# Half of a symmetric score matrix computed, the other half turned by the DMA crossbar: gated attention followed by a low-rank mixer

## The chip, the cores and the metric

One core of one Trainium2 chip runs the whole program. The metric is the device time of one execution in microseconds (us), smaller is better.

Engine names in the profile: PE is TensorE's matmuls, PEld its weight loads (which overlap matmuls), ACT is ScalarE, DVE is VectorE, POOL is GpSimd, SP is SyncE. A name with q (SPq, POOLq) is that engine's sequencer, which issues DMAs. L75 is a line of the kernel's file.

## The reference, cut to what matters

```python
# per batch of 8; S = 3136, D = 256, d_qk = 64, rank 32, hidden 1024
scores = (1 / S) * z @ z.T                 # symmetric
attn   = np.maximum(scores, 0) ** 2        # elementwise: symmetric too
x      = u * (attn @ v)
h      = (x.T @ U @ V).T                   # low rank, along the sequence
y      = x + h
out    = y + np.maximum(y @ w_ch1, 0) @ w_ch2
```

S is 24.5 tiles of 128, padded to 25. Each batch has an attention stage and a mixer stage.

## The kernel before

z, v and the weights are loaded as fp32 and cast by ScalarE. z and, later, x are transposed by matmuls with the identity. All 25 x 25 score blocks are computed, because the attention matmul needs each block with its contraction index on the partitions:

```python
for gi, (g0, gw) in enumerate(igroups):          # 512 query columns at a time
    for jp in range(0, NT, 2):
        for jj in range(npair):
            nc.tensor.matmul(out=ps_s[:, jj, :gw], lhsT=zzT[:, (jp+jj)*P : (jp+jj+1)*P],
                             rhs=zzT[:, g0 : g0 + gw], start=True, stop=True)
        # ReLU: 3 of 4 on ScalarE, 1 of 4 on VectorE; then the square on VectorE
    for q0 in range(0, gtiles, 2):
        for qq in range(nq):
            for jt in range(NT):
                nc.tensor.matmul(out=ps_o[:, qq, :], lhsT=attn_sb[:, jt, q*P : (q+1)*P],
                                 rhs=v_bf[:, jt, :], start=(jt == 0), stop=(jt == NT - 1))
        # x_bf = ps_o * u
...
# mixer: transpose x on TensorE and add V.T t1 in the same PSUM bank
for db in range(ND):
    for q in range(ctiles):
        nc.tensor.matmul(out=ps_u2[:, db, q*P : (q+1)*P],
                         lhsT=x_bf[:, it, db*P : (db+1)*P], rhs=ident, start=(q == 0), stop=False)
    nc.tensor.matmul(out=ps_u2[:, db, :cw], lhsT=t1_sb[:, db*P : (db+1)*P],
                     rhs=V_bf[:, c0 : c0 + cw], start=False, stop=True)
nc.scalar.copy(out=u2T_bf[:, :, c0 : c0 + cw], in_=ps_u2[:, :, :cw])
# then, per 512 columns: up (w1, ReLU on ScalarE) and down (w2)
```

## Time and profile before

| | before |
|---|---|
| median | 1374.6 us |
| TensorE matmuls busy | 1317.1 of 1373.0 us |
| first matmul | 19.7 us |
| one batch later on, attention + mixer | 106.2 + 61.7 us |
| issue of DMAs by SyncE | 288 plain loads and stores of 0.37 us each (median) |

Lines of the page of the kernel before: the span, each engine's busy time with its share of the span, two of the rows in which the span is cut in 40 slices (in tenths), and the shares of the chain of waits that ended last.

```profile
span 1373.0 us, 22895 instructions
PE 1317.1 (96%) x9865; PEld 913.3 (67%) x10008; DVE 707.9 (52%) x1104; ACT 792.9 (58%) x976; POOL 23.7 (2%) x41
...
PE   3999999999999999999999999999999999999998
...
DMA  9611421124111241111411115111121111111101
...
PE 75%; ACT 21%; DMA 2%; issue 1%; DVE 1%; ACTq 0%; SPq 0%; POOL 0%
```

TensorE is full in all slices but the first and the last, and the DMA engines are nearly empty outside loads.

Pieces of the chain that ended last, in order of time (start, length, what):

```profile
154.69 3.78 ACT relu_sb L277 x4
...
162.39 0.86 PE ps_1642 L270 x4
...
210.53 3.06 PE ps_2069 L202 x28
```

A matmul of 256 columns costs 3.06 / 28 = 0.109 us, one of 512 columns 0.86 / 4 = 0.215 us. In the same trace, matmuls of 128, 256 and 512 columns that follow one another without a gap start 55.5, 109.2 and 215.5 ns apart. So TensorE is paid per column streamed, 0.417 ns each, plus 2 to 3 ns a matmul.

Two stretches of the kernel before, attention and mixer of batch 1 (stretch, length, busy time of each engine with its instruction count, the granted clock, the DMA engines' busy share, GB/s), and its longest TensorE wait (total, times, longest):

```profile
196.90:303.10 106.20, 104.98 (x786) 74.18 (x797) 78.61 (x123) 55.35 (x69) 0.31 (x1) 1.00 0.10 29
303.10:364.80 61.70, 59.34 (x449) 39.69 (x455) 9.88 (x16) 42.61 (x53) 1.89 (x3) 1.00 0.40 123
```

```profile
PE ps_124 L128 <- ACT z_bf L121: 19.7, 1, 19.7
```

The attention starts of batches 1 and 7 lie at 196.9 and 1205.9 us in the timeline, so a batch takes (1205.9 - 196.9) / 6 = 168.2 us, and 1373.0 - 8 x 168.2 = 27.7 us lie outside eight such batches: the start and the end.

### The profile page before, as it was taken

The numbers are of one execution on the slowest core, as the hardware profiler recorded it, in microseconds if no ns is written. First come the engines' busy times: TensorE is split into PE (matmuls) and PEld (weight loads), VectorE is DVE, ScalarE is ACT, GpSimd is POOL, SyncE is SP. The second block draws the span as 40 slices with busy tenths as digits, with TensorE's granted clock in tenths as the row PEclk, the third lists the DMA queues.
The fourth block names the chain that finished last, engine by engine and source line by source line (L and its number), as shares of the span: only waits on it lengthen the run. The fifth ranks groups of instructions, "written<-read, shape, count | busy, mean of one in ns | idle before, by whom it ended". The sixth has DMA issues, their size and how long they took to land.

```text
span 1373.0 us, 22895 instructions
## 1 busy us (share of the span) xinstructions
PE 1317.1 (96%) x9865; PEld 913.3 (67%) x10008; DVE 707.9 (52%) x1104; ACT 792.9 (58%) x976; POOL 23.7 (2%) x41
## 2 busy tenths in 40 slices
PE   3999999999999999999999999999999999999998
PEld 1677666676666766667666676666766667666665
DVE  1776147751477414774157732677217772177721
ACT  6854855557555575556655565655655555455554
POOL 2000000000000000000000000000000000000000
PEclk9999999999999999999999999999999999999999
DMA  9611421124111241111411115111121111111101
GB/s 238 181 32 30 146 71 32 32 64 134 49 32 32 65 146 43 31 32 57 148 49 32 32 49 157 41 32 32 57 102 33 32 32 34 62 34 32 32 32 65
DMA packets 109542, 87.89 MB, mean 64 GB/s; under 512 B 32832, under 2 KB 109120, under 8 KB 109440
## 3 DMA queue, kind: packets, MB, share of 16 engines
q1 hardware_dynamic: 109440, 86.41, 20.7%
q8 instruction: 78, 1.28, 0.4%
q14 instruction: 24, 0.20, 0.0%
HBM read 60.70 MB, written 25.69 MB: 63 GB/s over the span
## 4 chain that ended last, share of the span: by engine, by line
PE 75%; ACT 21%; DMA 2%; issue 1%; DVE 1%; ACTq 0%; SPq 0%; POOL 0%
ACT relu_sb L277 12%; ACT attn_sb L184 4%; ACT u2T_bf L260 3%; ACT zzT L135 2%; DMA v_raw<-in_v_dram 1%; PE ps_6060 L202 0%; PE ps_4297 L202 0%; PE ps_11349 L202 0%; PE ps_7477 L202 0%; PE ps_2188 L202 0%; PE ps_12766 L202 0%; PE ps_11003 L202 0%; PE ps_9240 L202 0%; PE ps_5714 L202 0%; PE ps_2534 L202 0%
## 5 line engine op out<-in xcount | busy, mean ns | idle before, releaser
L202 PEld LDWEIGHTS <-attn_sb 128*128 128x128 bf16 x5000 | 466.9, 98 | 164.3 <-DVE attn_sb L189 61.9
L189 DVE TENSOR_TENSOR attn_sb<-attn_sb 128x1024 bf16<-128x1024 bf16 (+3 forms) x728 | 407.0, 608 | 73.7 <-ACT attn_sb L184 71.4
L169 PEld LDWEIGHTS <-zzT 128*128 128x128 bf16 x1400 | 133.3, 98 | 107.2 <-issue 29.3
L297 PEld LDWEIGHTS <-relu_sb 128*128 128x128 bf16 x1600 | 148.6, 98 | 50.5 <-ACT relu_sb L277 24.0
L270 PEld LDWEIGHTS <-w_bf 128*128 128x128 bf16 x896 | 83.2, 98 | 87.2 <-issue 7.8
L150 ACT CAST v_bf<-v_raw 128x1024 bf16<-128x1024 f32 (+1 forms) x56 | 52.0, 965 | 24.0 <-DMA v_raw<-in_v_dram 15.5
L246 PEld LDWEIGHTS <-x_bf 128*128 128x128 bf16 x400 | 30.3, 97 | 10.7 <-issue 4.5
L128 PEld LDWEIGHTS <-z_bf 128*128 128x128 bf16 x200 | 16.1, 102 | 26.3 <-issue 22.5
L289 PEld LDWEIGHTS <-V_bf 128*128 128x128 bf16 x200 | 19.3, 98 | 6.4
L223 PEld LDWEIGHTS <-U_bf 128*128 128x128 bf16 x200 | 19.6, 98 | 2.2
L212 POOL MEMSET u_sb<- 128x256 f32 x8 | 2.5, 311 | 1047.3 <-DVE x_bf L214 1047.3
L128 PE MATMUL ps_124<-ident,z_bf 128*128 128x128 bf16 x4 | 0.6, 299 | 19.7 <-ACT z_bf L121 19.7
L120 POOL MEMSET z_bf<- 128x1600 bf16 x8 | 11.4, 1431 | 80.8 <-PE ps_6732 L253 13.6
L121 ACT ACTIVATE z_bf<-z_raw 128x1600 bf16<-128x1600 f32 x8 | 12.4, 1550 | 0.0
L253 PEld LDWEIGHTS <-t_sb 128*128 128x128 bf16 x112 | 10.9, 97 | 1.4 <-issue 1.1
L305 DVE TENSOR_TENSOR out_sb<-ps_1522,x_bf 128x512 f32<-128x512 f32 x1 | 0.7, 692 | 16.8 <-PE ps_1522 L297 16.8
L305 DVE TENSOR_TENSOR out_sb<-ps_6811,x_bf 128x512 f32<-128x512 f32 x1 | 0.7, 692 | 16.7 <-PE ps_6811 L297 16.7
L305 DVE TENSOR_TENSOR out_sb<-ps_8574,x_bf 128x512 f32<-128x512 f32 x1 | 0.7, 692 | 16.7 <-PE ps_8574 L297 16.7
L305 DVE TENSOR_TENSOR out_sb<-ps_5048,x_bf 128x512 f32<-128x512 f32 x1 | 0.7, 690 | 16.7 <-PE ps_5048 L297 16.7
L305 DVE TENSOR_TENSOR out_sb<-ps_10337,x_bf 128x512 f32<-128x512 f32 x1 | 0.7, 692 | 16.7 <-PE ps_10337 L297 16.7
L305 DVE TENSOR_TENSOR out_sb<-ps_3285,x_bf 128x512 f32<-128x512 f32 x1 | 0.7, 690 | 16.7 <-PE ps_3285 L297 16.7
L305 DVE TENSOR_TENSOR out_sb<-ps_12100,x_bf 128x512 f32<-128x512 f32 x1 | 0.7, 690 | 16.7 <-PE ps_12100 L297 16.7
(2728 smaller groups left out, 2817.8 us busy)
## 6 DMA issues: line engine op xcount, KB each, us to landing
v_raw<-in_v_dram SPq DMA_DIRECT2D x48, 512.0 KB, 4.8
u_sb<-in_u_dram SPq DMA_DIRECT2D x96, 256.0 KB, 2.6
out_dram<-out_sb SPq DMA_DIRECT2D x96, 256.0 KB, 2.1
z_raw<-in_z_dram SPq DMA_DIRECT2D x8, 768.0 KB, 5.3
wtmp<-in_moe_w_ch_dram SPq DMA_DIRECT2D x4, 512.0 KB, 3.8
v_raw<-in_v_dram SPq DMA_DIRECT2D x8, 64.0 KB, 2.2
u_sb<-in_u_dram SPq DMA_DIRECT2D x8, 64.0 KB, 2.1
out_dram<-out_sb SPq DMA_DIRECT2D x8, 64.0 KB, 2.0
```

The costliest lines, as they stand in the source:

```text
L135: nc.scalar.copy(out=zzT[:, tg * P : (tg + n_in_g) * P], in_=pz[:, : n_in_g * P],)
L150: nc.scalar.copy(out=v_bf[:, c0 : c0 + cn, :], in_=v_raw[:, :cn, :])
L169: nc.tensor.matmul(out=ps_s[:, jj, :gw], lhsT=zzT[:, (jp + jj) * P : (jp + jj + 1) * P], rhs=zzT[:, g0 : g0 + gw], start=True, stop=True,)
L184: nc.scalar.activation(out=attn_sb[:, jp : jp + npair, :gw], in_=ps_s[:, :npair, :gw], func=AF.Relu,)
L189: nc.vector.tensor_tensor(out=attn_sb[:, jp : jp + npair, :gw], in0=attn_sb[:, jp : jp + npair, :gw], in1=attn_sb[:, jp : jp + npair, :gw] ...
L202: nc.tensor.matmul(out=ps_o[:, qq, :], lhsT=attn_sb[:, jt, q * P : (q + 1) * P], rhs=v_bf[:, jt, :], start=(jt == 0), stop=(jt == NT - 1),)
L223: nc.tensor.matmul(out=pt1[:, 0, :], lhsT=U_bf[:, it, :], rhs=x_bf[:, it, :], start=(it == 0), stop=(it == NT - 1),)
L246: nc.tensor.matmul(out=ps_u2[:, db, q * P : (q + 1) * P], lhsT=x_bf[:, it, db * P : (db + 1) * P], rhs=ident, start=(q == 0), stop=False,)
L260: nc.scalar.copy(out=u2T_bf[:, :, c0 : c0 + cw], in_=ps_u2[:, :, :cw])
L270: nc.tensor.matmul(out=ps_m1[:, hh, :cw], lhsT=w1_bf[:, db, ht * P : (ht + 1) * P], rhs=u2T_bf[:, db, c0 : c0 + cw], start=(db == 0), stop ...
L277: nc.scalar.activation(out=relu1_sb[:, hp : hp + 2, :cw], in_=ps_m1[:, :, :cw], func=AF.Relu,)
L297: nc.tensor.matmul(out=ps_f[:, qq, :], lhsT=relu1_sb[:, ht, q * P : (q + 1) * P], rhs=w2_bf[:, ht, :], start=False, stop=(ht == NH - 1),)
```

## The change

Because attn is symmetric, only blocks on and above the diagonal are computed. Row j of them is one score row `A[j]`. The block that attention tile o needs from below the diagonal is the transpose of a block of `A[o]`: one crossbar DMA turns the whole row into a "strip". z and x are transposed by DMA too; v, z and the weights are cast by the DMA that loads them (issued by GpSimd); the matmuls have a written order that mixes the scores for tile o + 3 into the attention of tile o. The rank product uses 32-column weights in four column groups. The core of the diff, with cuts:

```diff
+    AHEAD = 3
-    for dd in range(ND):
-        nc.sync.dma_start(out=wtmp, in_=moe_w_ch1[dd * P : (dd + 1) * P, :])
-        nc.scalar.copy(out=w1_bf[:, dd, :], in_=wtmp)
+    def load_z(b):
+        load_rows(nc.gpsimd, z_bf, z[b], dqk)          # fp32 to bf16 by the DMA
+        nc.sync.dma_start_transpose(out=zT[b % 2]..., in_=z_bf...)
+    load_z(0)
+    load_v(0)                                          # gpsimd, casts
+    nc.gpsimd.dma_start(out=w1_bf, in_=moe_w_ch1...)   # and w2, U, V
...
+    def score_steps(b, j):                             # blocks (j, j..24) only
+        ...  mm(out=ps[:, i, :h], lhsT=zt[:, j*P : (j+1)*P], rhs=zt[:, j*P + c0 ...])
+        nc.scalar.activation(out=dst, in_=ps[:, :parts, :h], func=AF.Relu, scale=sc)
+        nc.vector.tensor_tensor(out=dst, in0=dst, in1=dst, op=ALU.mult)
+        def turn():
+            strip = strip_pool.tile([P, NT - 1, P], BF16, name="strip")
+            nc.sync.dma_start_transpose(out=strip[:, : NT - 1 - j, :], in_=A[j][:, P:])
...
+            if j <= o:  w = A[j][:, (o - j) * P : (o - j + 1) * P]
+            else:       w = strips[o][:, j - o - 1, :]
+            mm(out=ps[:, q*D : (q+1)*D], lhsT=w, rhs=v_bf[:, j, :], ...)
...
+                for t in range(t0, t0 + nq):
+                    nc.sync.dma_start_transpose(out=uT[:, :, t*P : (t+1)*P], in_=x_bf[:, t, :])
...
+        for o in range(NT):
+            ahead = o + AHEAD
+            _spread(attend_steps(b, o), score_steps(b, ahead) if ahead < NT else [])
```

## The prediction

> **What bounds the kernel now.** TensorE. Page part 1: matmul busy 1317.1 of 1373.0 us (96%), ScalarE 58%, VectorE 52%. The chain of waits is 75% TensorE, 21% ScalarE (mostly the mixer's ReLU, 12%). The granted clock is 0.999: nothing to win there. The chain view gives the rate: 28 attention matmuls of 256 columns take 3.06 us, 109 ns each; four of 512 columns take 0.86 us, 215 ns each. TensorE is paid by columns streamed, 0.42 ns each, plus about 2.5 ns a matmul. Per batch I count about 371,000 columns: attention times v 160,000, scores 80,000, down 57,600, up 51,200, 6,400 each for rank, V and x transposes, 3,200 for z transposes. Eight batches: about 1262 us. The rest: about 20 us until the first matmul (timeline) and about 86 us lost, near 11 us a batch, where PSUM eviction lags (in the mixer the chain shows four ReLUs in a row, 3.78 us).
>
> **What the change does.** Scores fall to the upper triangle (40,000 columns); z and x transposes leave TensorE; padding columns go. About 320,000 columns a batch: 1068 us + 8,700 matmuls at 2.5 ns = about 1090 us. Saving about 170 us, all on the bounding engine. ScalarE loses the casts (52.0 us for v) and the x and z evictions; score ReLU halves but goes wholly to ScalarE (about 40 x 0.95 us a batch); squaring (0.6 us per 1024 columns) halves. Neither becomes a bound.
>
> **What it adds.** DMA transposes of 300 score blocks, 50 x blocks, 25 z blocks of 32 KB: 12.3 MB a batch, 98 MB in all, from one queue. This trace has no such DMA. The Trainium skill, "DMA: Bandwidth & Descriptors", section "Latency and other measured facts", gives 261 GB/s for non-contiguous transposes; no run here shows it yet. Demand is uneven: in the first attention windows TensorE needs about 2.7 us (attention) + 1.2 us (one score strip), and the queue must turn up to 21 blocks (690 KB) plus two x blocks: about 190 GB/s. Three strips of lead are some 8 us of slack. At 261 GB/s it fits; at 150 GB/s I estimate 5 to 8 us of stall a batch; the mean need is about 90 GB/s. I expect something between: about 30 us in all.
>
> Cast loads move to GpSimd and have a whole mixer phase (about 50 us) for v. The startup stays near 25 us (GpSimd memsets, z load, z transpose, three strips paced by ScalarE). The written order mixes scores into attention and down into up: eviction losses fall from 11 to about 4 us a batch.
>
> **Sum:** 1090 + 25 startup + 5 tail + 30 transposes + 30 evictions = about 1180 us. Range 1125 to 1290. Chances: faster by over 2% 0.92, within 2% 0.03, slower 0.05.
>
> **What would show it.** Right: TensorE busy above 90% of a span near 1180; attention matmuls still 109 ns; no waits on score strips longer than a few us per batch, those in its first third; ScalarE below 65%. Wrong: attention matmuls waiting on strip DMAs throughout, a SyncE queue busy nearly all the time, DMA share near full while few GB/s move, the granted clock dropping in gaps.
>
> **What would make it wrong.** Above all a crossbar rate far below 150 GB/s: at 75 GB/s the transposes alone last about 1310 us and eat the gain. Second, SyncE issue time per transpose, since it issues in order and also carries the output stores. Third, late cast loads. On the low side, transposes fully hidden: about 1125 us.

## The result, and the profile after

1206.3 us median (1203.2 to 1209.0, 4 runs) against 1374.6 us; the ratio is 0.878, 95% interval 0.876 to 0.879. A ratio here is the mean time of one kernel's runs over that of the other's runs of the same rounds, so it is not quite the ratio of the medians.

The page of the changed kernel, the same lines as before, with the granted clock's row and the two DMA queues (packets, MB, share of 16 engines' span):

```profile
span 1201.4 us, 20972 instructions
PE 1096.9 (91%) x8752; PEld 844.1 (70%) x8800; DVE 420.8 (35%) x680; ACT 531.6 (44%) x649; POOL 134.9 (11%) x210
...
PE   0669999899998999999999999989999999999998
...
PEclk9889999999999999999999999999999999999999
DMA  9998792989939897596947969289783988559612
...
q1 hardware_dynamic: 423552, 124.05, 54.9%
q0 software_dynamic: 63680, 43.81, 24.8%
...
PE 74%; DMA 14%; ACT 4%; SPq 3%; issue 2%; DVE 1%; POOL 1%; ACTq 0%; DVEq 0%; POOLq 0%
```

TensorE is now empty for more than a slice (30 us each) at the start, and thinner in the next few. The DMA engines, nearly empty before, are busy almost throughout, and 14% of the chain is DMA where it had been 2%.

Four stretches of the changed kernel: attention of batch 0, attention and mixer of batch 1, attention of batch 2 (columns as before):

```profile
41.70:147.50 105.80, 87.08 (x706) 70.11 (x706) 32.53 (x58) 35.10 (x45) 10.87 (x14) 0.90 0.94 157
204.00:290.30 86.30, 82.40 (x707) 68.39 (x706) 30.73 (x55) 32.96 (x42) 8.91 (x12) 1.00 0.79 150
290.30:348.50 58.20, 54.15 (x391) 36.66 (x395) 21.77 (x30) 33.34 (x39) 6.53 (x10) 1.00 0.84 136
348.50:434.60 86.10, 82.17 (x706) 68.56 (x706) 30.72 (x55) 32.96 (x42) 7.65 (x11) 1.00 0.82 151
```

The attention starts of batches 1 and 7 are at 204.0 and 1061.5 us, so a steady batch takes 142.9 us (168.2 before). Outside eight such batches lie 1201.4 - 8 x 142.9 = 58 us (27.7 before). The change therefore gains 8 x 25.3 = 202 us in the batches and gives about 30 us back at the start. The first attention alone is 20 us longer than a later one, and its granted clock is 0.90: after the long waits TensorE runs slower for a while. The Trainium skill, "TensorE: Matmul & The Clock Gate", Part 1, says that an idle window brings TensorE back to half rate; this trace agrees: the granted clock is 0.50 from 43.4 to 53.6 us and from 70.7 to 80.9 us, and TensorE waited for strips from 42.0 to 47.7 and from 66.4 to 78.0 us. (A DMA share above 1 in a row of this kind means that packets' times overlap; such shares are only compared with one another.)

TensorE's longest waits in the changed kernel (what waited, what ended it, total, times, longest):

```profile
PE ps_160 L75 <- DMA zT_84<-z_bf: 34.7, 1, 34.7
PE ps_399 L75 <- DMA strip<-A_93: 11.6, 1, 11.6
PE ps_219 L75 <- DMA strip<-A_89: 5.7, 1, 5.7
PE ps_3443 L75 <- DMA strip<-A_94: 2.5, 1, 2.5
```

The names A_89 to A_113 are score rows 0 to 24, so A_93 is row 4. The first is the start itself, the next two lie in the first attention. Summed over the trace, waits on strips are 42.6 us, of which 18.4 lie in batch 0 (including the two above) and 2.3 to 4.3 in each later one.

DMA issues of the changed kernel (what, sequencer, times, KB each where known, median us from issue to landing):

```profile
v_bf<-in_v_dram POOLq DMA_DIRECT2D x32, 384.0 KB, 11.0
uT<-x_bf SPq DMA_TRANSPOSE x200, 3.8
z_bf<-in_z_dram POOLq DMA_DIRECT2D x8, 384.0 KB, 8.1
...
strip<-A_92 SPq DMA_TRANSPOSE x8, 5.2
...
strip<-A_109 SPq DMA_TRANSPOSE x8, 2.5
```

Row 3 (A_92) has 21 blocks of 32 KB to turn, row 20 (A_109) has 4. The 17 blocks between them take 2.7 us, 0.159 us a block, or 206 GB/s, on top of about 1.9 us that any transpose takes. (This is with the kernel's other transfers under way; the expectation of extra_issue has 214.)

SyncE's own row in the first windows of batch 3 (start, length of the issue, what):

```profile
497.74 3.31 SPq L172 DMA_TRANSPOSE strip<-A_92  x1
501.14 3.22 SPq L227 DMA_TRANSPOSE uT<-x_bf  x2
504.46 3.04 SPq L172 DMA_TRANSPOSE strip<-A_93  x1
507.60 2.99 SPq L172 DMA_TRANSPOSE strip<-A_94  x1
510.68 2.51 SPq L227 DMA_TRANSPOSE uT<-x_bf  x2
```

SyncE issues one transpose after another without a pause; in the attention of batch 1 it is issuing for 75.0 of 86.3 us. The surprise is the x transposes: two of them take 2.5 to 3.2 us of SyncE though each turns only two blocks. Over the trace the median issue of one is 1.24 us. A strip of 8 blocks or fewer takes about 1.2 us to issue as well, a long one about 3.2 us.

### The profile page after: what moved, and what is told of

Its sections match the earlier page's. It is cut to its first block, busy times and chain, and to the rows that moved or that the text cites. A ratio compares the mean times of both kernels' runs of the same rounds, so it can differ in the third digit from the quotient of the medians.

```text
span 1201.4 us, 20972 instructions
## 1 busy us (share of the span) xinstructions
PE 1096.9 (91%) x8752; PEld 844.1 (70%) x8800; DVE 420.8 (35%) x680; ACT 531.6 (44%) x649; POOL 134.9 (11%) x210
## 4 chain that ended last, share of the span: by engine, by line
PE 74%; DMA 14%; ACT 4%; SPq 3%; issue 2%; DVE 1%; POOL 1%; ACTq 0%; DVEq 0%; POOLq 0%
SPq L172 2%; DMA strip<-A_93 2%; DMA zT_84<-z_bf 2%; DMA strip<-A_94 2%; DMA strip<-A_97 2%; DMA strip<-A_95 1%; DMA strip<-A_99 1%; ACT A_90 L158 1%; ACT A_89 L158 1%; SPq L227 1%; DMA strip<-A_101 1%; DMA out_dram<-o_sb 1%; DMA strip<-A_89 1%; PE ps_219 L75 1%; ACT A_91 L158 1%
## 5 line engine op out<-in xcount | busy, mean ns | idle before, releaser
L75 PEld LDWEIGHTS <-strip 128*128 128x128 bf16 x2400 | 233.1, 98 | 102.9 <-DMA strip<-A_93 22.0
L75 PEld LDWEIGHTS <-relu 128*128 128x128 bf16 x1600 | 156.5, 98 | 33.1 <-issue 2.8
L193 POOL DMA_DIRECT2D u_sb<-in_u_dram x96 | 68.9, 723 | 590.0 <-DVE x_bf L220 548.5
L75 PEld LDWEIGHTS <-zT_84 128*128 128x128 bf16 x396 | 39.4, 100 | 53.2 <-DMA zT_84<-z_bf 34.7
L75 PEld LDWEIGHTS <-zT_85 128*128 128x128 bf16 x396 | 38.4, 98 | 17.6 <-issue 8.7
L164 DVE TENSOR_TENSOR A_89<-A_89 128x832 bf16<-128x832 bf16 (+1 forms) x32 | 18.2, 567 | 44.9 <-ACT A_89 L158 44.9
L75 PE MATMUL ps_160<-zT_84 128*128 128x416 bf16 x2 | 0.9, 540 | 34.7 <-DMA zT_84<-z_bf 34.7
L121 POOL DMA_DIRECT2D v_bf<-in_v_dram x32 | 26.5, 856 | 10.6 <-PE ps_10270 L75 5.7
L164 DVE TENSOR_TENSOR A_96<-A_96 128x768 bf16<-128x768 bf16 (+1 forms) x24 | 13.1, 547 | 38.5 <-ACT A_96 L158 38.5
L75 PEld LDWEIGHTS <-A_90 128*128 128x128 bf16 x192 | 18.8, 98 | 10.9
L75 PEld LDWEIGHTS <-A_89 128*128 128x128 bf16 x200 | 19.6, 98 | 9.6
L164 DVE TENSOR_TENSOR A_92<-A_92 128x960 bf16<-128x960 bf16 (+1 forms) x24 | 15.3, 636 | 28.5 <-ACT A_92 L158 28.5
L164 DVE TENSOR_TENSOR A_94<-A_94 128x832 bf16<-128x832 bf16 x24 | 14.2, 593 | 16.1 <-ACT A_94 L158 16.1
L75 PEld LDWEIGHTS <-A_91 128*128 128x128 bf16 x184 | 18.0, 98 | 2.1
L164 DVE TENSOR_TENSOR A_93<-A_93 128x896 bf16<-128x896 bf16 (+1 forms) x24 | 14.7, 614 | 11.6 <-ACT A_93 L158 11.6
L75 PEld LDWEIGHTS <-A_92 128*128 128x128 bf16 x176 | 17.2, 98 | 2.0
```

The lines of the kernel that those rows point to most:

```text
L75: ins = nc.tensor.matmul(**kw)
L121: nc.gpsimd.dma_start(out=v_bf[:, t0 : t0 + 6, :], in_=v[b, t0 * P : (t0 + 6) * P, :].rearrange("(t p) d -> p t d", p=P),)
L164: nc.vector.tensor_tensor(out=dst, in0=dst, in1=dst, op=ALU.mult)
L193: nc.gpsimd.dma_start(out=u_sb[:, :nq, :], in_=u[b, o * P : (o + nq) * P, :].rearrange("(t p) d -> p t d", p=P),)
```

## The experiments

Each ran in three rounds beside the kernel before, whose median was 1374.2 to 1374.6 us in every group. "Steady batch" is (start of attention in batch 7 minus that in batch 1) / 6, from each trace. The trace of z_gate spans 1248.0 us where the execution listed with its times took 1238.7, so its stages are about 0.7% long; the other traces are within 0.2%.

| run | median us | ratio to before (95%) | steady batch us |
|---|---|---|---|
| before | 1374.6 | 1 | 168.2 |
| the change | 1206.3 | 0.878 (0.876 to 0.879) | 142.9 |
| no_strips (wrong) | 1146.0 | 0.834 (0.833 to 0.836) | 138.1 |
| uT_pairs | 1190.8 | 0.866 (0.865 to 0.868) | 141.2 |
| ahead4 | 1199.5 | 0.872 (0.869 to 0.874) | 142.4 |
| load_gate | 1195.7 | 0.870 (0.869 to 0.871) | 143.7 |
| z_gate | 1239.4 | 0.902 (0.901 to 0.904) | 151.3 |
| extra_issue | 1434.3 | 1.043 (1.041 to 1.045) | 172.7 |
| tri_off | 1311.3 | 0.954 (0.953 to 0.956) | 158.7 |
| x_on_pe | 1183.6 | 0.861 (0.860 to 0.863) | 140.3 |
| order_off | 1201.6 | 0.875 (0.872 to 0.878) | 143.2 |
| best1 | 1178.3 | 0.858 (0.857 to 0.859) | 140.3 |
| best2 | 1171.2 | 0.853 (0.851 to 0.854) | 140.1 |
| best3 | 1178.1 | 0.857 (0.856 to 0.858) | 139.9 |

### no_strips: what all strip transposes cost

```diff
-                w = strips[o][:, j - o - 1, :]
+                w = A[o][:, (j - o) * P : (j - o + 1) * P]     # untransposed: wrong result
-        if j < NT - 1:                                         # issue the strip transpose
+        if False:
```

> The changed kernel without the score-strip transposes: the lower blocks are read untransposed from the same score rows, so the result is wrong on purpose; TensorE, ScalarE and VectorE work is unchanged. Theory 1 (the strips cost only the waits that the trace shows, 42.6 us in all, 17 of them in the first batch): the time falls from 1206 to about 1160 to 1170 us, the waits on strips vanish, and the first matmul still starts near 35 us. Rival (the strips' traffic also slows loads, output stores and evictions): well below 1150 us, with a shorter mixer as well.

Measured: 1146.0 us, 60 us less than the change: below the 1160 to 1170 us of theory 1, but not well below 1150 us as the rival had it. Attention of batches 0 and 1 and the mixer of batch 1, without strips:

```profile
41.60:123.10 81.50, 81.50 (x707) 68.89 (x706) 32.58 (x58) 34.87 (x45) 11.34 (x15) 1.00 0.45 84
179.60:261.10 81.50, 81.50 (x707) 68.88 (x706) 30.76 (x55) 32.96 (x42) 9.34 (x13) 1.00 0.28 67
261.10:317.70 56.60, 54.18 (x397) 36.70 (x395) 21.87 (x30) 33.33 (x39) 6.11 (x9) 1.00 0.54 99
```

Attention is 81.5 us in every batch and never idle: that is TensorE's own time for 160,000 + 31,000 columns, which the prediction's count gives as 81.4 us. The strips thus cost 24.3 us in the first attention and 3.5 to 4.8 in each later one (mean 4.3). The trace's waits (42.6 us) understate the loss. Between the two profiled spans lie 57.2 us; beside the waits, 5.6 are matmuls at the lower clock in the first attention (87.1 us busy, against 81.5 here), about 6 are longer busy time in the seven later attentions (82.2 to 82.4 us in the two shown), whose cause is not shown, and about 3 are in the mixers (56.6 against 57 to 58). So the rival of slower loads and evictions accounts for only a few us.

### uT_pairs: fewer issues, the same bytes

```diff
-                for t in range(t0, t0 + nq):
-                    nc.sync.dma_start_transpose(
-                        out=uT[:, :, t * P : (t + 1) * P], in_=x_bf[:, t, :])
+                nc.sync.dma_start_transpose(        # uT is now [P, NT, ND, P]
+                    out=uT[:, t0 : t0 + nq].rearrange("p t d c -> p (t d) c"),
+                    in_=x_bf[:, t0 : t0 + nq, :].rearrange("p t d -> p (t d)"))
```

The users of uT take the new layout; the last chunk of columns is padded from 320 to 384.

> The x transposes issued once for a pair of tiles, not once a tile: the same bytes, 13 issues a batch in place of 25 (each takes 1.24 us of SyncE now). It streams 64 padding columns more in the last chunk, about 4 us in all. Theory 2 (strips are late because SyncE issues back to back in the first half of attention): waits on strips fall from about 3.6 to about 1.5 us in a steady batch and the time falls by about 12 us net, to near 1194. Rival (the crossbar's rate sets the lateness): waits unchanged, time up by about 4 us.

Measured: 1190.8 us, 15.5 us less than the change despite the padding. Waits on strips in a steady batch are 1.0 to 2.2 us. SyncE's row in the first windows of batch 3:

```profile
495.54 1.22 SPq L226 DMA_TRANSPOSE uT<-x_bf  x1
496.85 6.92 SPq L172 DMA_TRANSPOSE strip<-A  x2
```

One issue of four blocks takes the 1.22 us that one of two blocks took. The bytes are unchanged and the waits of a steady batch are about halved, so the rival (the crossbar's rate alone) falls. The layout into which x is turned changed with the number of issues; what it does by itself was not tested.

### extra_issue: more issues, few bytes

```diff
                     nc.sync.dma_start_transpose(
                         out=uT[:, :, t * P : (t + 1) * P], in_=x_bf[:, t, :]
                     )
+                    nc.sync.dma_start_transpose(out=spare[t % 6], in_=x_bf[:, t, :])
```

> Every x transpose is issued a second time into a spare tile that nobody reads: 25 issues and 1.6 MB more a batch. Theory 2 (SyncE's issue time sets the lateness): 25 x 1.24 us = 31 us more of SyncE in an attention stage in which it is busy for about 70 of 86 us; attention grows by 15 to 25 us a batch and the time to 1330 to 1400 us. Rival (the crossbar's bytes): 1.6 MB at the 214 GB/s that I read from the landing times are 7.7 us a batch, so at most 60 us in all, under 1270 us.

Measured: 1434.3 us, slower than the kernel before. That is above my range, and far above the rival's. Attention of batch 1:

```profile
227.70:337.80 110.10, 87.94 (x708) 70.18 (x706) 30.70 (x56) 32.96 (x42) 7.65 (x11) 0.95 0.64 129
```

It grew from 86.3 to 110.1 us while the DMA engines' share fell from 0.79 to 0.64: more waiting with less moved a second. (1434.3 - 1206.3) / 200 added issues is 1.14 us each, nearly the 1.24 us that an issue takes. By the steady batch it is (172.7 - 142.9) / 25 = 1.19 us: nearly every issue is paid for in full, 24 us of it in the attention shown and the rest in the mixer. Some of this is the lower clock after waits (0.95 here, 87.9 us busy against 82.4). What stays open is where the fixed time arises, in SyncE's own work or in something behind it that makes SyncE wait; both look alike here.

### ahead4: a strip more of lead

```diff
-    AHEAD = 3
+    AHEAD = 4
-    strip_pool = ctx.enter_context(tc.tile_pool(name="strip", bufs=AHEAD + 1))
+    strip_pool = ctx.enter_context(tc.tile_pool(name="strip", bufs=AHEAD))
+            if c == 4:
+                mix = mix + nxt[3]
```

> Four score strips in place of three are computed ahead of the attention, with the same four strip buffers. Theory 2 and the rival both say that strips are late only because the demand of the first windows exceeds what the queue turns; a strip more of lead (about 3.7 us) should take the steady waits from about 3.6 us to under 1 us a batch: 1206 to about 1180 us. If the buffers are now what strips wait for, the waits stay.

Measured: 1199.5 us, a fall of 7 us where 26 were expected. Batches 1, 2 and 4 wait for strips for only 0.4 to 1.4 us, but batches 3 and 5 to 7 for 2.5 to 4.4 us, and waits on the output tile `o_sb` grew from 2.0 to 8.2 us. TensorE's waits of this run:

```profile
PE ps L75 <- DMA strip<-A: 27.7, 18, 8.0
...
PE ps L75 <- DVE o_sb L349: 8.2, 7, 2.2
```

The output stores stand behind strip transposes in SyncE's queue (before the wait of 2.2 us an output tile was ready at 730.9 us and its store was issued at 740.2, after two strips), so lead for the strips is partly taken from the mixer. Why only some batches gain was not settled.

### load_gate: the first z transpose without company

```diff
     load_z(0)
+    for t in list(range(0, NF, 6)) + [NF]:
+        nc.vector.tensor_copy(out=v_bf[:1, t, :1], in_=zT[0][:1, :1])   # v loads wait for zT
     load_v(0)
-    nc.gpsimd.dma_start(out=w1_bf, ...)        # w1, w2, U, V: the same, each held by a
+    (issued after attention tile 15)           # one-element copy from x tile 14
```

> In the first batch the v loads wait for the z transpose and the weight loads for the middle of the attention; nothing else is changed. Theory 3 (the prediction's startup was too small because the first z transpose shares the DMA engines with about 5 MB of cast loads: it took 21.5 us to land against 6.3 later): the first matmul starts near 20 us in place of 34.7 and the time falls by 10 to 15 us. Rival (the transpose is slow for its own sake when it comes first): the first matmul stays near 35 us or later.

Measured: 1195.7 us, 10.6 us less. The first z transpose of the changed kernel on SyncE's row, then the same of this run, then this run's longest single TensorE wait:

```profile
13.11 10.91 SPq L114 DMA_TRANSPOSE zT_84<-z_bf  x1
```

```profile
13.41 3.80 SPq L114 DMA_TRANSPOSE zT<-z_bf  x1
```

```profile
PE ps L75 <- DMA zT<-z_bf: 19.2, 1, 19.2
```

The same transpose takes 3.8 us to issue, not 10.9, and the first matmul starts at 19.2 us, not 34.7. The rival falls: the transpose was slow because the cast loads of v and the weights shared the DMA engines. Of the 15 us gained, about 5 went again: v now came late by 2.1 us, and the first attention took 108.2 us against 105.7.

### z_gate: the next z load moved

```diff
+            if more and o == 13:
+                nc.vector.tensor_copy(out=z_bf[:1, 0, :1], in_=x_bf[:1, 12, :1])
+                nc.vector.tensor_copy(out=z_bf[:1, NF, :1], in_=x_bf[:1, 12, :1])
+                load_z(b + 1)                   # in place of before tile 0
```

> The load of the next batch's z is held back until x tile 12 of the running batch is done; nothing else is changed. In the changed kernel two such loads (each about 3,100 packets of 128 to 256 bytes) fell into the first windows of the first batch, and a strip then took 10 to 12 us to land. Theory 3b (those two loads cause most of the first batch's strip waits of 18.4 us): the first batch's attention falls from 105.7 to about 92 us, and the time by 8 to 12 us; later batches hardly move. Rival (the first batch waits because its first strips start from nothing, with no mixer before them): waits stay above 15 us there.

Measured: 1239.4 us, slower by 33 us. The first attention did fall, from 105.7 to 99.2 us, half of what I expected; but in every later batch the load now fell among the strips. Attention of batch 1:

```profile
200.40:294.80 94.40, 85.66 (x707) 69.90 (x705) 30.89 (x57) 32.96 (x42) 10.71 (x15) 0.96 0.81 142
```

It is 94.4 us, 8.1 more than in the change; batch 7, after which no z is loaded, takes 85.3. A failed improvement, but it measures what the next z, only 0.8 MB, costs where it meets strips. In the change its load falls on the mixer. SyncE's row around the z transpose of this stage:

```profile
257.15 3.16 SPq L172 DMA_TRANSPOSE strip<-A  x2
264.70 4.44 SPq L114 DMA_TRANSPOSE zT<-z_bf  x1
```

The edit moved two things at once, and the trace shows both at work. The load was under way from 255.6 to 264.4 us, and the two strips issued beside it took 7.9 and 6.3 us to land; the same rows in batch 7 took 3.2 and 3.0. And the z transpose, which needs the loaded z, kept SyncE from 260.3 to 269.1 us: 4.4 us without an issue until the load had landed, then 4.4 us for its own issue, with the next strips behind it. TensorE waits twice, 2.9 and 2.6 us, once for a strip of each kind, and then runs at a lower clock (85.7 us busy against 82.4). So the load alone is not shown to cost the 8 us. The Trainium skill, "DMA: Bandwidth & Descriptors", section "Specifications", gives 512 B as the least size for line rate; z's rows are 256 B as fp32 and 128 B as bf16. No run here shows that the small rows matter: in the changed kernel z took 8.1 us to land, and v's pieces, about as many bytes each in rows of 1 KB, issued four in a row, took 11.0.

### tri_off: the lower half on TensorE

```diff
-            nc.sync.dma_start_transpose(out=strip[:, : NT - 1 - j, :], in_=A[j][:, P:])
+            for k in range(n):                  # 8 blocks at a time
+                i = j + 1 + k0 + k
+                mm(out=ps[:, k // 4, (k % 4)*P : (k % 4 + 1)*P],
+                   lhsT=zt[:, i*P : (i+1)*P], rhs=zt[:, j*P : (j+1)*P], ...)
+            # ReLU on ScalarE into the strip, square on VectorE
```

> The strips of lower blocks are computed on TensorE again (300 matmuls of 128 columns a batch, ReLU and square), in place of the crossbar transposes: the triangle alone undone. Without strip traffic the kernel takes 1146 us; the matmuls add 8 x 300 x 56 ns = 134 us if they stream back to back, or 235 us if each waits for its 98 ns weight load. So 1280 to 1390 us, and the crossbar's triangle is worth 75 to 180 us net. If the lower half were cheaper than the strip waits it would be under 1206 us.

Measured: 1311.3 us, within the range. Attention of batch 1:

```profile
209.50:303.90 94.40, 94.40 (x939) 81.74 (x937) 50.78 (x94) 61.63 (x81) 7.65 (x11) 1.00 0.25 57
```

No wait at all, but 12.9 us more than the 81.5 us without strips, for the 231 blocks that fall into this stage: 56 ns a block. The other 69 fall into the mixer, which takes 64.1 us against 56.6 without strips: 109 ns a block there. So the triangle by crossbar is worth 1311.3 - 1206.3 = 105 us; of the 165 us of work that it takes away (1311.3 - 1146.0) it gives back 60.

### x_on_pe: x transposed on TensorE again

```diff
-                for t in range(t0, t0 + nq):
-                    nc.sync.dma_start_transpose(out=uT[:, :, t*P : (t+1)*P], in_=x_bf[:, t, :])
...
+                for q in range(n):
+                    mm(out=ps[:, db, q*P : (q+1)*P], lhsT=x_bf[:, t0+q, db*P : (db+1)*P],
+                       rhs=ident, start=(q == 0), stop=False)
                 mm(out=ps[:, db, : n*P], lhsT=t1[b]..., rhs=V_bf..., start=False, stop=True)
-            nc.vector.tensor_tensor(out=dst, in0=ps[:, :, :w], in1=dst, op=ALU.add)
+            nc.vector.tensor_copy(out=uT[:, :, t0*P : t0*P + w], in_=ps[:, :, :w])
```

> x is transposed by TensorE again (50 matmuls of 128 columns a batch, accumulated with the V term in PSUM), not by DMA: that part alone undone. TensorE gains 2.8 to 4.9 us a batch. Theory 2: SyncE is freed of 25 issues of 1.24 us, so the strips come earlier and the attention falls from 86 to 82 to 83 us a batch; the two about cancel: 1190 to 1215 us. If the x transposes by DMA were free of side effects, the time would be up by the whole 22 to 39 us, to 1228 us or more.

Measured: 1183.6 us, 22.7 us less than the change, and better than I expected. Attention and mixer of batch 1:

```profile
200.10:281.60 81.50, 81.50 (x708) 68.87 (x706) 30.72 (x55) 32.99 (x42) 9.57 (x13) 1.00 0.72 141
281.60:340.00 58.40, 56.62 (x446) 39.47 (x445) 21.80 (x30) 33.45 (x39) 5.88 (x9) 1.00 0.81 132
```

Attention is at TensorE's own time again, with all strips still turned by the crossbar. The mixer's matmuls grew by 2.5 us (56.6 against 54.2 busy). Transposing x by DMA was a loss: it saved 2.5 us of TensorE a batch, and cost 3.9 us of attention in a later batch (mean of seven) and 6.6 in the first.

### order_off: without the written TensorE order

```diff
-        if last[0] is not None:        # dependency on the previous matmul
+        if False:
```

> The changed kernel without the written TensorE order: the scheduler orders TensorE by its own estimate of readiness, all else as in the changed kernel. If the written order is part of the gain, score and attention matmuls are no longer mixed as evenly and the time rises by 10 us or more, to 1216 us or above. If the scheduler does as well, 1196 to 1216 us; the strips, which the order cannot bring sooner, stay the limit.

Measured: 1201.6 us, with an interval that overlaps the change's. The written order is not shown to have any effect; here the scheduler does as well without it.

### best1, best2, best3: put together

best1 is x_on_pe with load_gate, and holds the second batch's z load until x tile 16 of the first batch. best2 also computes the next batch's first strip among the last attention tile's matmuls:

```diff
+            if o == NT - 1:
+                nxt = [score_steps(b + 1, j) if more else [] for j in range(AHEAD)]
+                _spread(attend_steps(b, o), nxt[0])
...
-            nc.scalar.copy(out=t1_sb, in_=ps[:, :D])
+            nc.vector.tensor_copy(out=t1_sb, in_=ps[:, :D])
```

best3 spreads the first batch's weight loads over x tiles 4 to 12.

> x transposed on TensorE, v loads of the first batch after the z transpose, weight loads and the second batch's z load held to the second half of the first batch's attention. The effects measured one by one should nearly add: 1183.6 us for x on TensorE, less 10 to 14 us for the earlier first matmul, less 6 to 10 us for the first batch's strip waits: 1160 to 1168 us. If the first batch's strip waits come only from starting with nothing computed ahead, the last part stays away: 1170 us or more.

> As best1, and the next batch's first score strip is computed among the last attention tile's matmuls, not alone after it, with the t1 copy moved from ScalarE to VectorE: in the changed kernel TensorE waits 2.4 us a batch there for ScalarE. It should take 1 to 2 us off a batch, 8 to 14 us in all: 1148 to 1160 us. If ScalarE's eviction then only makes a later matmul wait, the time is that of best1.

> As best2, but the first batch's weight loads are not let go together after x tile 14: they are spread one by one over x tiles 4 to 12, and the second batch's z load follows at tile 14. Together they held the z transpose until 126 us and its strips, so that the first mixer lost 4 to 9 us. If that bunching was the cause, the first mixer falls to about 57 us and the time to 1160 to 1167 us. If each of these loads costs its own time wherever it meets strips, the first attention grows by as much and the time stays near 1171 us.

Measured: 1178.3, 1171.2 and 1178.1 us. best1 missed its expectation by 10 us or more and lies in the other branch, 1170 us or more: the effects do not add. The loads that were taken out of the start came back at the end of the first attention and the start of the first mixer. There, too, the order of SyncE's queue shows: in best1 an output tile was ready at 150.8 us and its store was issued at 160.7, behind the z transpose and two strips, and TensorE then waited 6.8 us on `o_sb`. Attention and mixer of batch 0 and attention of batch 1 of best1, then of batch 0 of best2:

```profile
26.70:128.20 101.50, 86.88 (x706) 70.73 (x705) 33.67 (x68) 35.12 (x45) 16.97 (x23) 0.93 1.10 165
128.20:196.00 67.80, 59.19 (x447) 40.40 (x445) 21.82 (x30) 33.44 (x39) 8.06 (x11) 0.95 0.87 132
196.00:277.50 81.50, 81.50 (x707) 68.93 (x706) 30.73 (x55) 32.96 (x42) 9.49 (x13) 1.00 0.71 141
```

```profile
26.70:129.90 103.20, 88.75 (x713) 71.96 (x712) 34.84 (x70) 37.49 (x48) 18.32 (x25) 0.92 1.09 163
129.90:191.20 61.30, 57.24 (x441) 39.59 (x440) 21.25 (x29) 30.89 (x36) 6.70 (x10) 0.97 0.89 145
```

The first mixer takes 67.8 us where a later one takes 58.5. best2's gain over best1 is 7 us, most of it in that mixer (61.3); its steady batch is about the same (140.1 against 140.3), so moving the strip among the last tile's matmuls was not worth the 1 to 2 us a batch that I gave it. best3 was meant to mend the first batch and made it worse (attention 106.5, mixer 64.6): the bunching theory falls. The other branch, about 1171 us, is missed as well, by 7 us, so that each load simply costs its own time wherever it meets strips is not shown either. best2 is the fastest correct version that ran: 2.9% under the change, 14.8% under the kernel before.

## Why the prediction was right, and where it was off

It gave 1180 us with a range of 1125 to 1290, and faster by over 2% with a chance of 0.92; 1206.3 was measured. Point by point:

- **TensorE's work: right.** "About 1090 us" was counted from columns; without strips TensorE is busy for 1086.9 of 1144.2 us, and the attention takes the counted 81.5 us.
- **The steady batch: right in sum.** The prediction has (1090 + 30 + 30) / 8 = 143.8 us a batch; 142.9 was measured. Within it two errors cancel, which is luck: without strips the batch is 4.8 us shorter (3.8 predicted for transposes), and what then remains above TensorE's own 135.9 us is 2.2 (3.8 predicted for evictions). The strip waits were said to lie in the first third of the stage; of 24.2 us in the later batches 17.1 do.
- **"Startup near 25 us" plus a tail of 5: the step that failed.** In its place are 58 us outside eight steady batches: 41.7 until the first attention, 19 more in the first batch than in a steady one, and 3 less at the end. The prediction costed the start by memsets, the z load, its transpose and three strips, each as if alone; late cast loads it named only as a risk. It did not see that several MB of cast loads would be in flight at the same time (load_gate: 15 us of first matmul), nor that the first windows' strips would meet further loads and then a lower clock (24.3 us lost to strips in the first attention, 4.3 later). In the 11.6 us wait for row 4, the next z transpose held SyncE from 59.9 to 64.5 us just before that strip, and the z load after it ran beside the strip, which took 10.7 us to land (5.4 in the median).
- **"Transposes 30 us": off by half.** no_strips shows 60 us; the excess is in that same first batch.
- **The crossbar's rate: right in kind.** It was said to lie between 150 and 261 GB/s; 206 GB/s was read.
- **"SyncE issue time per transpose": named only as a risk, and given no term.** It is what makes strips late in a steady batch, as far as these runs separate it from something behind SyncE that makes it wait: uT_pairs takes issues away and halves the waits, extra_issue adds them and pays 1.14 us each. Two signs that the prediction had listed as "wrong" did show: a SyncE queue busy nearly all the time (75.0 of 86.3 us) and, in the first attention, a lower granted clock (0.90). A consequence was missed: transposing x by DMA is a loss (x_on_pe).
- **Evictions "from 11 to about 4 us a batch": not separated.** The mixer's named waits are 2.4 us a batch on ScalarE, but the order that was to bring the gain has no effect of its own (order_off).
- **ScalarE below 65%, TensorE above 90%: right,** 44% and 91%.

Not isolated: the z transposes by DMA and the casts by DMA, each by itself, in the steady batch. Why best2 still has about 50 us outside the steady batches (1170.2 - 8 x 140.1) is only partly shown: strip 0, which the first tile needs whole, and the loads of v and weights all want the same DMA engines then.

## What to carry to other kernels

Moving work from a full engine to idle DMA pays when the work is large (here half of a score matrix, 105 us); small transposes pay a fixed time each, so put several blocks into one or leave them on TensorE. Cost the start on its own: what is hidden in every later batch can all be exposed at once in the first one. When one queue issues in order, look at what each issue waits for: a transpose that waits for its load, or that is long to issue, holds up the strips and stores behind it (z_gate, best1).

## What the Trainium skill lacked or had wrong

- "DMA: Bandwidth & Descriptors", section "DMA Transpose (X-bar)", gives no fixed cost for a transpose; the page's only issue time of a DMA transpose, in sequencer cycles, stands in its part on trn3, for "previous generations". Here one takes about 1.2 us of SyncE to issue for 1 to 8 blocks of 128 x 128 bf16 (plain issues 0.37 us), and at least 2.3 us to land.
- "Advanced Engine Details and Errata", section "X-Bar Transpose (TRN2)", says that transposes are as fast as regular DMAs and expects 350 to 400 GB/s; "DMA: Bandwidth & Descriptors", section "Latency and other measured facts", has 261 GB/s for the non-contiguous case. SBUF to SBUF here: 206 GB/s beyond the fixed time, with the kernel's other transfers under way.
- No page gives what a load costs the transposes beside it: here a strip of 8 or 7 blocks took 5.5 to 9.1 us to land beside a load of 0.8 MB of z, and 3.2 or 3.0 us in the batch without such a load (z_gate).
- "TensorE: Matmul & The Clock Gate", section "Back-to-back issue gap", gives about 81 ns a matmul for a stream of weight loads and matmuls of 128 columns. Here such matmuls, mixed with ones of 256 columns, added 56 ns each in the attention; in the mixer, with the waits there, 109 ns (tri_off).
